# The vector, scalar and GpSimd queues of an MoE and MLP kernel written out by hand, and the gate's short products moved between tiles

## The chip, the cores and the metric

The kernel runs on one core of a Trainium2 chip. The metric is the device time of one execution in microseconds (us), lower is better. The core has five engines that matter here: TensorE (PE, matrix products), VectorE (DVE), ScalarE (ACT), GpSimd (POOL) and SyncE (SP, which issues the DMA transfers). Each engine takes its instructions in a fixed order, and an instruction at the head of a queue that waits for another engine holds back all that stands behind it.

## The reference, cut to what matters

```python
def attention(q, k, v):            # 2 x 8 heads, 576 positions, 64 wide
    out_d = sm_attn(q_d, k_d, v_d) # on means of 4 positions
    out_local = softmax(where(|i - j| < 4, q k^T / 8, -1e9)) @ v
    return repeat(out_d, 4) + out_local

def moe(x, w_gate, w1, w2):        # x: 1152 x 512, 8 experts, hidden 1024, float32
    P = exp(x @ w_gate - max)
    for _ in range(8):
        P /= P.sum(1, keepdims=True) + 1e-09
        P /= P.sum(0, keepdims=True) + 1e-09
        P *= N / E
    return sum(P[:, e:e+1] * (maximum(x @ w1[e], 0) @ w2[e]) for e in range(E))

def mlp(x, w_in, w_out):           # hidden 2048; w_in and w_out are float64
    return log(1 + exp(x @ w_in)) @ w_out
```

The three follow each other: attention gives the MoE's x, the MoE gives the MLP's.

## The kernel before

**Precision.** Each float32 operand is split into a high part (`h`, cut by a cast) and the rest (`l`), and each product is made as three: high by high, high by low, low by high. The splits are the work of ACT (casts), DVE and POOL (subtractions).

**Steps.** The MoE and the MLP are one list of 80 steps, a step being one slice of 256 hidden columns of one expert (the MLP counts as experts 8 and 9) for one of the two sets of tokens: s=0 is four tiles of 128 tokens (half: 256 columns), s=1 five tiles (half: 320). Steps 0 to 3 run beside the attention, the main loop from step 4 (the fifth step); steps 64 to 79 are the MLP. A step has **first products** (`first`, line 577): seven products of a Strassen-like scheme on half blocks, of six matmuls (line 601) each, and **second products** (`second`, line 649), one group of six matmuls of 512 columns (line 660) for each tile. The first products of step n+2 are written between the tiles of step n, so between two of a step's products there is as a rule one tile of second products. Only PE's order is written by hand (`manual_schedule` in the main loop); the queues of DVE, ACT, POOL and SP are set by the scheduler of the framework.

**Between the products.** The first products share three banks of PSUM. Three of them are copied out by ACT (`t1`, `t5`, `u2`: line 610, called the t and u copies below), and PE may write the bank again only after the copy. Three combines on DVE (`c11`, `c22`, `c12`: line 615) add the next products to these copies. `hidden` makes the hidden values: in the MoE a Relu on ACT (line 558, `hh`) and the low part on DVE (line 559, `hl`); in the MLP eight instructions for log(1 + exp(x)) on ACT, DVE and POOL (lines 564 to 575). The second products accumulate in PSUM and are added to the rows with the gate's factor on DVE (`weigh`, line 677).

**Weights.** Each slice of an expert's weights is loaded raw (`raw`, a pool of two buffers) and split: `fetch_first` for w1 (loads `raw<-in_moe_w`, casts lines 132 and 138, subtractions lines 133 and 139, four sums of blocks on POOL, line 111), `fetch_second` for w2 (casts line 153, subtractions line 154). They are issued three slices ahead.

**float64 weights.** `convert` (line 162) turns one of 32 pieces of the float64 weights into float32 high and low parts with integer operations (lines 178 to 189, on `cva`), splits it (lines 196 and 197) and stores it to a scratch in DRAM (`s_in`, `s_out`), from where the MLP steps load it ready. It is called from step 12 on, two pieces in three steps.

**Gate.** `gates` (line 464) makes the logits before the main loop, and nine short products (line 482, `lg`, 18 matmul records) turn them by tiles. Then `sinkhorn` runs in pieces, one after each tile of second products from step 4 on: the row part is four small DVE instructions (lines 503 to 506), then a product on PE sums the columns (line 509, `m<-pr,ones`), and four more on DVE (lines 511 to 516).

**Turn to the MLP.** `again` (line 680) transposes the MoE's result on PE, copies it out on ACT (line 693, `xf`) and makes the seven operands of the first products for each of two halves `kk` (`operands`: casts line 241, subtractions line 242).

Of the kernel before, what the change touches and what calls it, by code (L numbers as in the profile page):

```python
# [20 lines left out]
def attention_moe_mlp(ctx: ExitStack, tc: tile.TileContext, q, k, v, w_gate, w1, w2, w_in, w_out, out):  # L21
# [30 lines left out]
    OPS = 7  # L52

# [6 lines left out]
    tmpp = ctx.enter_context(tc.tile_pool(name="tmpp", bufs=11))  # L60
# [11 lines left out]
    def tmp(s, name):  # L72
        return tmpp.tile([P, HALF[1]], F32, tag="t", name=name)[:, : HALF[s]]
# [29 lines left out]
    weights = {}  # L103
# [9 lines left out]
    def fetch_first(f, n):  # L113
        e, p = divmod(n, NP)
# [7 lines left out]
        raw = rawp.tile([P, 2, 2, 2, P], F32, tag="raw", name="raw1")  # L122
# [5 lines left out]
        for part, src in (  # L128
            (slice(SUMS, SUMS + 1), raw[:, 0:1, :, 0, :]),
            (slice(SUMS + 1, OPS), raw[:, 1].rearrange("p k f c -> p f k c")),  # L130
        ):
            nc.scalar.copy(hi[:, part], src)
            nc.vector.tensor_tensor(lo[:, part], src, hi[:, part].bitcast(F32), op=ALU.subtract)
        two = [smp.tile([P, 2, 2, P], F32, tag="sums", name="sums") for _ in range(2)]
        weight_sums([two[i // 2][:, i % 2] for i in range(SUMS)], lambda fh, d: raw[:, d, :, fh, :])
        for i, sums in enumerate(two):
            part = slice(2 * i, 2 * i + 2)
            nc.scalar.copy(hi[:, part], sums)  # L138
            nc.gpsimd.tensor_tensor(lo[:, part], sums, hi[:, part].bitcast(F32), op=ALU.subtract)  # L139

    def fetch_second(f, n):
# [8 lines left out]
        raw = rawp.tile([P, 2, DM], F32, tag="raw", name="raw2")  # L150
        nc.sync.dma_start(raw, w2[e].rearrange("(h a p) d -> p h a d", h=2, p=P)[:, :, p, :])
        for i in range(2):
            nc.scalar.copy(hi[:, i], raw[:, i])  # L153
            nc.gpsimd.tensor_tensor(lo[:, i], raw[:, i], hi[:, i].bitcast(F32), op=ALU.subtract)  # L154


    TINY = 2.0 ** -15 * 1.125

    HALVES = F2 // P

    def convert(i):

        raw = rawp.tile([P, 2, 2, 2 * P], U32, tag="raw", name="raw64")
# [13 lines left out]
        a = smp.tile([P, SUMS * P], U32, tag="sums", name="cva")  # L177
# [399 lines left out]
    def first(n):  # L577
# [16 lines left out]
        def product(i, b=None):  # L594
            more = b is not None
            if not more:
                b = bank(places[i], f"m{i}")
# [261 lines left out]
```

## Time and profile before

| what | us |
|---|---|
| three runs, median (lowest to highest) | 1095.36 (1095.34 to 1096.3) |
| span of the profiled execution | 1094.7 |
| the median less this span | 0.66 |
| PE busy, share of the span | 1060.0, 97% |
| DVE busy | 727.0, 66% |
| ACT busy | 555.2, 51% |
| POOL busy | 537.6, 49% |

The profiled execution's own time is its span; what lies around it is taken as the 0.66 us by which the median of the runs is longer. PE's busy time counts matmuls that overlap, so idle time, and late starts from one matmul to the next, are what tells of lost time. In the trace, a name in front of `<-` is what an instruction writes and the names behind it what it reads; the bracket at the end is the time that its engine sat idle before it and what ended this.

### The profile page before, as it was taken

The numbers are of one execution on the slowest core, as the hardware profiler recorded it, in microseconds if no ns is written. First come the engines' busy times: TensorE is split into PE (matmuls) and PEld (weight loads), VectorE is DVE, ScalarE is ACT, GpSimd is POOL, SyncE is SP. The second block draws the span as 40 slices with busy tenths as digits, with TensorE's granted clock in tenths as the row PEclk, the third lists the DMA queues.
The fourth block names the chain that finished last, engine by engine and source line by source line (L and its number), as shares of the span: only waits on it lengthen the run. The fifth ranks groups of instructions, "written<-read, shape, count | busy, mean of one in ns | idle before, by whom it ended". The sixth has DMA issues, their size and how long they took to land.

```text
span 1094.7 us, 17873 instructions
## 1 busy us (share of the span) xinstructions
PE 1060.0 (97%) x6385; PEld 938.0 (86%) x6385; DVE 727.0 (66%) x1532; ACT 555.2 (51%) x1443; POOL 537.6 (49%) x569
## 2 busy tenths in 40 slices
PE   6899999999999999999999999999999998999998
PEld 5678888998987889888888988898898897889987
DVE  6889665565666676667657665766663578766765
ACT  4667645343444444434444443444443567676763
POOL 6735235464467676756766455354664212222321
PEclk9579999999999999999999999999999999999999
DMA  8454101111235334434443332223333273244112
GB/s 175 118 115 109 49 27 55 62 58 40 84 100 145 115 110 143 132 105 127 122 134 102 117 112 93 100 93 110 102 116 116 106 278 139 113 175 182 68 39 87
DMA packets 133497, 119.70 MB, mean 109 GB/s; under 512 B 35744, under 2 KB 111776, under 8 KB 133408
## 3 DMA queue, kind: packets, MB, share of 16 engines
q1 hardware_dynamic: 133408, 118.56, 35.0%
q8 instruction: 50, 0.82, 0.3%
q14 instruction: 39, 0.32, 0.1%
HBM read 93.11 MB, written 25.43 MB: 108 GB/s over the span
## 4 chain that ended last, share of the span: by engine, by line
PE 40%; POOL 5%; DMA 5%; DVE 3%; issue 2%; ACT 2%; SPq 0%; POOLq 0%; ACTq 0%; DVEq 0%
PE yps L660 21%; PE m L601 19%; DMA raw<-in_moe_w_out 2%; POOL sums L111 2%; POOL w2l L154 1%; POOL cva L188 1%; POOL cva L197 1%; DMA raw<-in_moe_w 1%; DMA raw<-in_moe_w_in 1%; DVE cva L178 1%; POOL w1l L139 1%; DVE cva L189 0%; DVE cva L179 0%; DVE cva L182 0%; DMA s_out<-cva 0%
## 5 line engine op out<-in xcount | busy, mean ns | idle before, releaser
L601 PE MATMUL m<-xh,w1h 128*128 128x320 f32 (+1 forms) x1120 | 336.6, 301 | 13.1 <-ACT t L610 6.3
L601 PE MATMUL m<-xh,w1l 128*128 128x320 f32 (+1 forms) x1120 | 332.5, 297 | 0.0
L601 PE MATMUL m<-xl,w1h 128*128 128x320 f32 (+1 forms) x1120 | 332.4, 297 | 0.0
L601 PEld LDWEIGHTS m<-xh,w1h 128*128 128x128 f32 x1120 | 212.2, 189 | 38.7 <-ACT t L610 10.8
L601 PEld LDWEIGHTS m<-xl,w1h 128*128 128x128 f32 x1120 | 212.4, 190 | 11.8
L601 PEld LDWEIGHTS m<-xh,w1l 128*128 128x128 f32 x1120 | 212.2, 190 | 0.2 <-issue 0.2
L660 PE MATMUL yps<-w2h,hh 128*128 128x512 f32 x502 | 198.5, 395 | 0.0
L660 PE MATMUL yps<-w2l,hh 128*128 128x512 f32 x502 | 198.4, 395 | 0.0
L660 PE MATMUL yps<-w2h,hl 128*128 128x512 f32 x502 | 195.5, 389 | 0.0
L660 PE MATMUL yps<-w2h,h 128*128 128x512 f32 x436 | 153.3, 393 | 0.0
L615 DVE TENSOR_TENSOR c<-m,t 128x256 f32<-128x256 f32 (+1 forms) x160 | 72.3, 452 | 100.9 <-PE m L601 99.5
L139 POOL TENSOR_TENSOR w1l<-sums,w1h 128x512 fp32r<-128x512 f32 x72 | 95.8, 1345 | 78.2 <-ACT w1h L138 54.4
L571 POOL TENSOR_TENSOR ab<-ab,up 128x320 f32<-128x320 f32 (+1 forms) x64 | 53.9, 843 | 157.2 <-ACT ln L567 109.8
L154 POOL TENSOR_TENSOR w2l<-raw,w2h 128x512 fp32r<-128x512 f32 x72 | 94.9, 1339 | 71.4 <-ACT w2h L153 71.3
L558 ACT ACTIVATE hh<-c 128x256 fp32r<-128x256 f32 (+1 forms) x138 | 60.0, 443 | 125.0 <-DVE c L615 123.3
L559 DVE SCALAR_TENSOR_TENSOR hl<-c,hh 128x256 fp32r<-128x256 f32 (+1 forms) x138 | 91.4, 668 | 35.0 <-ACT hh L558 33.2
L660 PEld LDWEIGHTS yps<-w2h,hl 128*128 128x128 f32 x502 | 94.4, 188 | 21.3
L677 DVE SCALAR_TENSOR_TENSOR acc<-yps,pr,acc 128x512 f32<-128x512 f32 x117 | 86.9, 743 | 29.5 <-PE yps L660 29.4
L660 PEld LDWEIGHTS yps<-w2h,hh 128*128 128x128 f32 x502 | 94.7, 189 | 12.6 <-DVE acc L673 0.2
L660 PEld LDWEIGHTS yps<-w2l,hh 128*128 128x128 f32 x502 | 94.7, 189 | 11.1 <-issue 0.4
L660 PEld LDWEIGHTS yps<-w2h,h 128*128 128x128 f32 x436 | 82.6, 189 | 14.8
L188 POOL TENSOR_TENSOR cva<-cva,raw 128x512 uint32<-128x512 uint32 x32 | 42.7, 1336 | 95.2 <-DVE raw L185 76.6
(134 smaller groups left out, 1700.7 us busy)
## 6 DMA issues: line engine op xcount, KB each, us to landing
raw<-in_moe_w SPq DMA_DIRECT2D x72, 256.0 KB
raw<-in_moe_w SPq DMA_DIRECT2D x36, 512.0 KB
w1h<-s_in SPq DMA_DIRECT2D x10, 896.0 KB
w1l<-s_in SPq DMA_DIRECT2D x10, 896.0 KB
raw<-in_moe_w_in SPq DMA_DIRECT2D x32, 256.0 KB
raw<-in_moe_w_out SPq DMA_DIRECT2D x16, 512.0 KB
w2l<-s_out SPq DMA_DIRECT2D x10, 512.0 KB
w2h<-s_out SPq DMA_DIRECT2D x10, 512.0 KB
```

Source lines behind the costliest of these rows:

```text
L111: nc.gpsimd.tensor_tensor(sums[i], a, b, op=op)
L139: nc.gpsimd.tensor_tensor(lo[:, part], sums, hi[:, part].bitcast(F32), op=ALU.subtract)
L154: nc.gpsimd.tensor_tensor(lo[:, i], raw[:, i], hi[:, i].bitcast(F32), op=ALU.subtract)
L178: nc.vector.tensor_scalar(a, high, 0x07FFFFFF, 3, op0=ALU.bitwise_and, op1=ALU.logical_shift_left)
L188: nc.gpsimd.tensor_tensor(a, a, low, op=ALU.add)
L558: nc.scalar.activation(hh, c, AF.Relu)
L559: nc.vector.scalar_tensor_tensor(out=hl, in0=c, scalar=0.0, in1=hh.bitcast(F32), op0=ALU.max, op1=ALU.subtract)
L571: nc.gpsimd.tensor_tensor(ab, ab, up, op=ALU.subtract)
L601: nc.tensor.matmul(b[:, :h], x[:, i, kk, :], y[s][:, i, kk, :], start=(not more and n == 0), stop=(n == 5), skip_group_check=more,)
L615: nc.vector.tensor_tensor(c, b[:, :h], t, op=ALU.add)
L660: nc.tensor.matmul(y, a[:, f, tok], b[:, f, :], start=(start and m == 0), stop=(stop and m == 5))
L677: nc.vector.scalar_tensor_tensor(out=acc[t], in0=y, scalar=pr[:, t, e : e + 1], in1=acc[t], op0=ALU.mult, op1=ALU.add,)
```

## The change

1. **Queues by hand.** A planner (`Order`, with a `Job` for each chain of instructions) keeps a clock for each engine, in which each instruction has a duration written in the code (0.35 to 1.35 us). After each product and each tile it issues the instructions that, by its clock, can start before PE's next piece is done; on ACT and DVE only those that end within 0.6 us (`SLACK`) after it. The copies and combines that PE's products need are put at their places directly. ACT's, DVE's and POOL's order is fixed in this way from step 4 to step 61 (`turned[1] - 2` is 62); from there the scheduler sets it again. SP stays with the scheduler in the whole kernel.
2. **Conversions.** They begin at step 4 instead of 12, one at a time, as the planner finds room. Two of a conversion's DVE instructions are gone (lines 179 and 185 of before), and one ACT instruction is added (a Copy of the low words with scale 2^-29; its value is added by POOL's addition as before). Per kernel: 64 DVE instructions fewer, 32 on ACT more; POOL, PE and SP as many as before.
3. **Buffers.** The raw pool of two buffers becomes two pools of one: in the main loop the weights use one, the conversions the other (in the attention w1 the one, w2 the other). The conversions' `cva` get a pool of their own (`lowp`), which the MLP's `up` shares; `ln` moves to the pool of the sums.
4. **Gate.** The nine short products go from in front of the main loop to step 4, three after each of three tiles, with a copy after each three; the Sinkhorn pieces begin three tiles later, and in the ninth step (n = 8) two pieces follow each tile.
5. **`again`.** The operands are made for all of the first half `kk`, then all of the second, with every subtraction on DVE.

From the main loop on, PE's order is the same but for the gate's products. In the attention stage the scheduler still sets all queues; with the other pools it comes to another order there (PE's first differs at its 180th row; on SP the loads of w2 stand earlier, those of w1 later), with the same work.

```diff
-    rawp = ctx.enter_context(tc.tile_pool(name="rawp", bufs=2))
+    rawp = [ctx.enter_context(tc.tile_pool(name=f"raw{i}", bufs=1)) for i in range(2)]
...
+    class Order:
+
+        SLACK = 0.6
...
+        def one(self, end):
+            best = None
+            for job in self.jobs:
+                at_ = None if job.active else self.begin(job)
+                if at_ is None:
+                    continue
+                last = end if job.want[0] in ("POOL", "DMA") else end + self.SLACK - job.want[1]
+                key = at_ + 0.25 * job.rank
+                if at_ <= last and (best is None or key < best[0]):
+                    best = key, job
...
+    LOAD, LANDS = 2.0, 2.2
...
+        bits = yield "ACT", 0.69, t
+        nc.scalar.activation(low, low, AF.Copy, scale=2.0 ** -29)
+        t = yield "DVE", 0.6, t
         nc.vector.tensor_scalar(a, high, 0x07FFFFFF, 3, op0=ALU.bitwise_and, op1=ALU.logical_shift_left)
-        nc.vector.scalar_tensor_tensor(
-            out=a, in0=low, scalar=29, in1=a, op0=ALU.logical_shift_right, op1=ALU.bitwise_or
-        )
+        t = yield "DVE", 0.8, t
         nc.vector.scalar_tensor_tensor(
             out=a, in0=high, scalar=0xC0000000, in1=a, op0=ALU.bitwise_and, op1=ALU.bitwise_or
         )
-        nc.vector.tensor_scalar(low, low, 28, 1, op0=ALU.logical_shift_right, op1=ALU.bitwise_and)
...
+    def logits(shares):
+        for t0 in range(0, NTT, LOGITS):
+            lg = spare[0][:, HALF[1] : HALF[1] + LOGITS * E]
+            for t in range(t0, t0 + LOGITS):
+                nc.tensor.matmul(
+                    lg[:, (t - t0) * E : (t - t0 + 1) * E], shares[:, t * P : (t + 1) * P], fold, start=True, stop=True
+                )
+            nc.vector.tensor_copy(prf[:, t0 * E : (t0 + LOGITS) * E], lg)
+            yield
+        nc.vector.tensor_reduce(m1, prf, axis=AX.X, op=ALU.max)
+        yield from sinkhorn()
...
-        for i in ORDER:
-            for kk in range(2):
-                yield from operands(s, kk, xf[kk], (i,), [nc.vector if i in FASTI else nc.gpsimd])
+        for kk in range(2):
+            split[s].append(order_.add(operands(s, kk, xf[kk], ORDER, [nc.vector], order_.free["ACT"]), 1))
...
-    CV = 12
+    CV = 4
...
+                for _ in range(0 if not m else 2 if n == ends[0, 1] + 1 else 1):
```

Three places show what moves (line numbers are each kernel's own: 610 of before is 821 of the change, 615 is 828, 153 is 292, 196 is 346). The first is ACT in front of the first products of step 46, whose t and u copies are the `COPY` rows with 128x320; rows with `raw_` and `cva` are a conversion's, `w2h` are casts of w2. Before:

```order
L558 ACTIVATE h_7313<-c_7355 128x256
L558 ACTIVATE h_7313<-c_7372 128x256
L186 ACTIVATE raw_7423<-raw_7423 128x512
L558 ACTIVATE h_7313<-c_7389 128x256
L558 ACTIVATE h_7313<-m_7315 128x256
L153 CAST w2h<-raw_7417 128x512 x2
L196 CAST raw_7423<-cva 128x512
L610 COPY t_7450<-m_7443 128x320
L610 COPY t_7459<-m_7452 128x320
```

With the change:

```order
L737 ACTIVATE h_7235<-c_7285 128x256
L292 CAST w2h<-raw_7255 128x512 x2
L737 ACTIVATE h_7235<-c_7304 128x256
L737 ACTIVATE h_7235<-c_7326 128x256
L737 ACTIVATE h_7235<-m_7237 128x256
L346 CAST raw_7073<-sums 128x512
L346 CAST raw_7073<-cva 128x512
L821 COPY t_7376<-m_7367 128x320
L821 COPY t_7393<-m_7378 128x320
```

The casts of w2 stand three Relus earlier, and the conversion next to the copies is an older one, at its last two casts, while before it was one whose casts followed on its first instructions in the same step.

The second is DVE at the Sinkhorn pieces beside step 8 (`c_` and `hl` or `h_` rows are the combines and the low parts, `grs` and `pr` the row part, `gcs` and `pr` the column part). Before:

```order
L615 TENSOR_TENSOR c_2796<-m_2789,t_2762 128x256
L559 SCALAR_TENSOR_TENSOR h_2754<-c_2796,h_2753 128x256
L511 TENSOR_REDUCE gcs<-m_2789 128x8
L514 TENSOR_SCALAR gcs<-gcs 128x8
L515 RECIPROCAL gcs<-gcs 128x8
L615 TENSOR_TENSOR c_2820<-m_2755,t_2771 128x256
L516 SCALAR_TENSOR_TENSOR pr<-pr,gcs 128x72
L503 TENSOR_REDUCE grs<-pr 128x9
L504 TENSOR_SCALAR grs<-grs 128x9
L559 SCALAR_TENSOR_TENSOR h_2754<-c_2820,h_2753 128x256
L505 RECIPROCAL grs<-grs 128x9
L506 TENSOR_TENSOR pr<-pr,grs 128x72
```

With the change:

```order
L828 TENSOR_TENSOR c_2955<-m_2946,t_2915 128x320
L739 SCALAR_TENSOR_TENSOR hl<-c_2955,hh 128x320
L680 TENSOR_REDUCE grs<-pr 128x9
L681 TENSOR_SCALAR grs<-grs 128x9
L682 RECIPROCAL grs<-grs 128x9
L683 TENSOR_TENSOR pr<-pr,grs 128x72
L688 TENSOR_REDUCE gcs<-m_2946 128x8
L691 TENSOR_SCALAR gcs<-gcs 128x8
L692 RECIPROCAL gcs<-gcs 128x8
L693 SCALAR_TENSOR_TENSOR pr<-pr,gcs 128x72
L828 TENSOR_TENSOR c_2987<-m_2907,t_2926 128x320
L828 TENSOR_TENSOR c_2996<-m_2917,u_2944 128x320
```

The row part and the column part, which had a combine and a low part between them, now follow each other directly, and PE's product `m<-pr,ones` between them comes right after the tile.

The third is ACT at the turn to the MLP, in front of the first products of step 66 (`xf` are copies of the transposed rows, `xh_` casts of operands, `ab`, `ln` and `hh` hidden values; the copies `t_` are again what PE waits for). Before:

```order
L610 COPY c_9964<-m_9820 128x320
L564 ACTIVATE ab<-c_9964 128x320
L574 CAST hh<-ab 128x320
L565 ACTIVATE ab<-ab 128x320
L567 ACTIVATE ln<-ab 128x320
L610 COPY t_10007<-m_10000 128x320
L610 COPY t_10016<-m_10009 128x320
```

With the change:

```order
L821 COPY c_9941<-m_9797 128x320
L767 CAST hh<-ab 128x320
L932 COPY xf_9872<-tp 128x2x128
L932 COPY xf_9873<-tp 128x2x128
L752 ACTIVATE ln<-ab 128x320
L748 ACTIVATE ab<-ab 128x320
L746 ACTIVATE ab<-c_9941 128x320
L821 COPY t_9984<-m_9977 128x320
L821 COPY t_9993<-m_9986 128x320
L406 CAST xh_103<-xf_9872 128x256
```

The last two copies `xf` now stand behind `c_9941`, and the casts `xh_`, six of which stood among the rows ahead of the t copies, stand behind them: from the first `xf` copy to `t_` there are 21 rows where there were 27.

## Rows read from the trace of the kernel before

**Rows 1.** Windows: stretch, length, busy time of PE, PEld, DVE, ACT, POOL, granted clock.
```profile
0.00:165.00 165.00, 146.70 (x1101) 123.50 (x1101) 126.51 (x345) 102.10 (x388) 79.91 (x108) 0.88 0.44 99
205.00:853.00 648.00, 639.02 (x3680) 568.70 (x3680) 414.09 (x729) 275.75 (x610) 375.03 (x370) 1.00 0.34 107
530.00:660.00 130.00, 129.91 (x759) 116.71 (x760) 86.26 (x150) 57.69 (x128) 75.36 (x72) 1.00 0.38 118
```
**Rows 2.** Windows of line 188 alone (POOL, one instruction in each conversion): length, busy (count).
```profile
530.00:660.00 130.00, 9.28 (x7) 1.00 0.38 118
```
**Rows 3.** Waits of PE, 165 to 853 us: for what, us in total, times, longest.
```profile
PE m L601 <- ACT t L610: 3.9, 6, 1.2
```
**Rows 4.** Timeline of PE at step 46: start, us, instruction, idle before it.
```profile
665.52 0.39 PE L660 MATMUL yps<-w2l,hh 128*128 128x512 f32 x1
665.75 0.39 PE L660 MATMUL yps<-w2h,hl 128*128 128x512 f32 x1
667.35 0.42 PE L601 MATMUL m<-xh,w1h 128*128 128x320 f32 x1 [1.20 <-ACT t L610]
667.60 0.31 PE L601 MATMUL m<-xl,w1h 128*128 128x320 f32 x1
667.75 0.31 PE L601 MATMUL m<-xh,w1l 128*128 128x320 f32 x1
```
**Rows 5.** Timeline of ACT at the same place.
```profile
666.35 0.62 ACT L196 CAST raw<-cva 128x512 fp32r<-128x512 f32 x1 [1.50 <-DVE cva L189]
666.88 0.75 ACT L610 COPY t<-m 128x320 f32<-128x320 f32 x2
```
**Rows 6.** Groups of DVE and ACT by line, 205 to 853 us: busy, mean ns | idle before.
```profile
L178 DVE TENSOR_SCALAR cva<-raw 128x512 uint32<-128x512 uint32 x32 | 28.6, 892 | 49.8 <-DMA raw<-in_moe_w_out 18.3 <-POOL w1l L139 17.4 <-DMA raw<-in_moe_w_in 14.0
L179 DVE SCALAR_TENSOR_TENSOR cva<-raw,cva 128x512 uint32<-128x512 uint32 x32 | 22.5, 702 | 0.7
L186 ACT ACTIVATE raw<-raw 128x512 f32<-128x512 f32 x32 | 21.9, 684 | 53.2 <-DVE cva L182 49.2 <-DMA raw<-in_moe_w 4.0
L558 ACT ACTIVATE hh<-c 128x320 fp32r<-128x320 f32 x57 | 26.1, 470 | 48.9 <-DVE c L615 48.9
L559 DVE SCALAR_TENSOR_TENSOR hl<-c,hh 128x320 fp32r<-128x320 f32 x57 | 42.4, 757 | 13.6 <-ACT hh L558 12.3
L615 DVE TENSOR_TENSOR c<-m,t 128x320 f32<-128x320 f32 x56 | 27.1, 484 | 49.7 <-PE m L601 48.6 <-ACT u L610 1.0
```
**Rows 7.** Line 178 at 339 and 523 us, duration in ns; POOL's timeline there.
```profile
L178 DVE TENSOR_SCALAR cva<-raw x1: 1503/1503/1503, 339.1 to 339.1; 128x512 uint32<-128x512 uint32 x1
...
L178 DVE TENSOR_SCALAR cva<-raw x1: 427/427/427, 523.6 to 523.6; 128x512 uint32<-128x512 uint32 x1
...
337.76 2.52 POOL L139 TENSOR_TENSOR w1l<-sums,w1h 128x512 fp32r<-128x512 f32 x2
...
525.88 1.29 POOL L188 TENSOR_TENSOR cva<-cva,raw 128x512 uint32<-128x512 uint32 x1 [2.80 <-DVE raw L185]
```
**Rows 8.** Chain that ended last, 300 to 700 us: longest landing of a load.
```profile
654.78 4.67 DMA raw<-in_moe_w_out
```
**Rows 9.** Timeline of PE: the nine short products in front of the main loop.
```profile
164.75 2.17 PE L482 MATMUL lg<-fold,lts 16*128 16x8 f32 x18
```
**Rows 10.** Timelines of DVE and PE at a Sinkhorn row part.
```profile
184.52 0.22 DVE L503 TENSOR_REDUCE grs<-pr 128x9 f32<-128x72 f32 x1
...
185.55 0.23 DVE L506 TENSOR_TENSOR pr<-pr,grs 128x72 f32<-128x72 f32 x1
...
185.93 0.30 PE L509 MATMUL m<-pr,ones 128*128 128x72 f32 x1 [0.46 <-DVE pr L506]
```
**Rows 11.** The turn to the MLP: timelines of ACT and PE, then the clock.
```profile
915.08 0.73 ACT L610 COPY t<-m 128x320 f32<-128x320 f32 x2
...
915.54 0.41 PE L601 MATMUL m<-xh,w1h 128*128 128x320 f32 x1 [2.42 <-ACT t L610]
...
916.00:920.00 4.00, 4.00 (x16) 3.68 (x15) 2.42 (x6) 2.28 (x5) 0.82 (x1) 0.57 0.00 0
```

More of the change, by code (lines that the diff above doesn't have):

```diff
@@ L70, in attention_moe_mlp, with tmp @@
     turns = count()
-    def tmp(s, name):
+    held = []
+    class Mark:
+        want = True
+    def tmp(s, name, owner=None):
+        if order_.on:
+            if len(held) >= TEMPS and held[-TEMPS]:
+                old = held[-TEMPS]
+                assert isinstance(old, Job) or not old.want, name
+                order_.force(old)
+            held.append(owner or order_.running)
         return tmpp.tile([P, HALF[1]], F32, tag="t", name=name)[:, : HALF[s]]
@@ L101, in attention_moe_mlp, with __init__, go @@
     s_out = scratch("s_out", [F2 // (2 * P), 2, P, 2, DM])
-    weights = {}
+    weights, fetching = {}, {}
+    class Job:
+        def __init__(self, steps, rank):
+            self.steps, self.rank, self.want, self.active, self.taken, self.done = steps, rank, None, False, {}, set()
+            self.last = 0.0
+            self.go(None)
+        def go(self, value):
+            before, order_.running = order_.running, self
+            self.active = True
+            try:
+                self.want = self.steps.send(value)
+            except StopIteration:
+                self.want = None
+            self.active, order_.running = False, before
@@ L596, in product @@
             if not more:
+                if i == 5 and step - 1 in making:
+                    order_.force(making[step - 1][-1][1])
                 b = bank(places[i], f"m{i}")
+            for job in split[s] if e >= E else ():
+                while job.want and i not in job.done:
+                    order_.step(job)
+                    order_.now = max(order_.now, job.last)
             n = 0
@@ L681, in again @@
     def again(s, banks):
+        assert s or not any(job.taken.get("raw") or job.rank == 2 for job in order_.jobs)
         if s:
@@ L685, in again @@
         else:
-            xf = [rawp.tile([P, 2, 2 * HALF[s]], F32, tag="raw", name="xf2") for _ in range(2)]
+            xf = [x.tile([P, 2, 2 * HALF[s]], F32, tag="raw", name="xf2") for x in rawp]
         for i, t in enumerate(TILES[s]):
@@ L781, in attention_moe_mlp, with conversions @@
     ahead[turned[1] - 2] = [turned[1] - 1, turned[1]]
-    balance, pending, pieces = sinkhorn(), None, 0
+    balance, pending = logits(shares), None
+    def conversions():
+        t = 0.0
+        for e in range(2):
+            for kind in range(2):
+                for i in range(HALVES // 2):
+                    t = yield from convert(kind * HALVES + e * HALVES // 2 + i, t)
     def leading(ns):
@@ L789, in leading @@
             yield from lead(n)
+    others = ExitStack()
     with tc.manual_schedule(engines={mybir.EngineType.PE}):
+        order_.on = True
+        others.enter_context(
+            tc.manual_schedule(engines={mybir.EngineType.Activation, mybir.EngineType.DVE, mybir.EngineType.Pool})
+        )
         for n in range(BESIDE, len(steps)):
+            if n == turned[1] - 2:
+                order_.on = False
+                others.close()
+                for job in order_.jobs:
+                    while job.want:
+                        job.go(0.0)
+                order_.jobs.clear()
+            if n == CV:
+                order_.add(conversions(), 2)
             e, g, s, p = steps[n]
@@ L812, in attention_moe_mlp @@
                     weigh(e, s, i, ys[i])
[L813 to L814 removed]
+                for _ in range(0 if not m else 2 if n == ends[0, 1] + 1 else 1):
+                    if not balance:
+                        break
+                    order_.did("DVE", 0.6)
+                    if next(balance, True):
+                        balance = None
+                        for t in range(NTT):
+                            scaled[t] = order_.add(scale_rows(t))
                 for _ in range(PIECES):
```

244 lines of the change are left out of this document (200 added, 44 removed).

## The prediction

> **What bounds the kernel now.** I read the windows by stage first, then PE's waits, then one wait closely on each engine. In the main stretch, 205 to 853 us, PE is busy 639.02 of 648 us at a granted clock of 1.00 [rows 1]: TensorE is the bound, and what this change could at most give back there is the time in which PE stands. Its printed idle time is 648 - 639.02 = 9.0 us. It isn't spread evenly: from 530 to 660 us PE stood 0.09 of 130 us, and the 130 us from 710 to 840 read the same (130.00 busy). The waits behind the idle time are mostly those for ACT's t and u copies, 3.9 us in six waits for the t copies alone, and then for DVE's combines [rows 3]. So PE does not lack work of its own; a copy comes late now and then.
>
> Why it comes late is to be seen at step 46. PE waits 1.20 us for the t copy [rows 4]. ACT had been idle for 1.50 us before the cast of line 196, which waited for a conversion's instruction on DVE, and the t copies stand right behind this cast [rows 5]. The copy was ready to run; its queue was blocked by work that nobody needs for hundreds of us. In PE's timeline I count 17 late starts of this kind from 205 to 853 us; behind nearly all stands a conversion, or a split of weights, in the queue of ACT or DVE.
>
> A late start costs more than its printed idle time. At step 46 the last second product begins at 665.75 and the next matmul at 667.35, 1.60 later where the pace is 0.23 (665.52 to 665.75): 1.37 lost against 1.20 printed. And the first matmul after the wait takes 0.25 to the next (667.35 to 667.60) where the pace is 0.15 [rows 4]: 0.10 more. So each costs 0.27 over what is printed, and the 17 together 9.0 + 17 x 0.27 = 13.6 us.
>
> **The change part by part.** The sum is made against the span of the profiled execution, 1094.7; the median of the runs is 0.66 above it.
>
> Queues by hand: the mechanism acts at the right place. The planner lets ACT and DVE begin a conversion's instruction only if, by its clock, it ends within 0.6 us after PE's piece, so it should not stand waiting ahead of a t copy. A t copy has a tile and a product's time until PE needs its bank, which is what the order before also gave where nothing stood in front. If all 17 go: -13.6. What remains of them, or comes new, is not in the trace. The bounds: below by 0, since PE's busy time can't shrink; above by 13.6, the same rate as now. The nearest row is the stretch from 530 to 660 us, which had seven conversions in it [rows 2], as has the one from 710 to 840, one in 18.6 us; the changed kernel spreads 32 over some 640 us, one in 20. Those stretches lost 0.1 us, so conversions at this pace fit beside the products if they fall right. But the planner's durations are fixed numbers: it gives line 178 0.6 us, where the trace has a mean of 0.89 [rows 6], and a load 4.2 us to land, where the longest in the chain takes 4.67 [rows 8]. I take 3 us, nearer to the clean stretches than to the rate of now.
>
> Conversions: the removed instruction of line 179 took 0.70 us, 22.5 us in all, and the other removed one comes on top; the added one on ACT is of the size of line 186, 0.68 us, so 32 x 0.68 = 22 us [rows 6]. DVE is busy 414.09 and ACT 275.75 of 648 us [rows 1], so both have room, and neither sum lies on the path: 0. What hides the added ACT work is the idle time of ACT behind PE; where that cover is gone, it is a late t copy of 0.68 us plus 0.27, which is inside the 3 us.
>
> The Trainium skill, "ScalarE: Activation LUTs", "Rules for kernel authors", would have plain arithmetic on DVE rather than ACT; by that rule this edit goes the wrong way. The row of the form on ACT (0.68) is shorter than that of the DVE instruction it replaces (0.70), so the trace doesn't bear the rule out here.
>
> Gate: the nine short products took 2.17 us in front of the loop [rows 9] and take the same between tiles, where PE is the bound too: 0, within the 0.1 of a restart for each of three groups. The Sinkhorn pieces begin three tiles later and are made up in step 8 by two pieces per tile, and there a wait is added: PE's column product comes right after the tile, and needs the row part. Before the row part DVE's queue holds the combine and the low part, which waits for ACT's Relu: 0.48 + 0.47 + 0.76 us [rows 6]. The row part itself ran from 184.52 to 185.78 with a low part of about 0.4 inside [rows 10], so 0.85 to 1.0 alone. From the end of the product this is 2.7 us, and one tile, six times 0.23 = 1.38, runs beside it: PE waits 1.3, and twice so, each with the 0.27: +3.2. Bounds: 0 if the Relu and the low part were passed earlier than the rows say, 5 if the column part also holds back the combines behind it in DVE's queue (c and t banks that PE needs next). The wait at 185.93 (0.46, with its 0.27) goes, as the pieces are elsewhere: -0.7. Together +2.5.
>
> Raw buffers: weights now have one buffer, so a load can't start before the last subtraction of the load before. The price is a rival's, below; the forecast has 0, since one load of weights comes per step (some 53 steps lie in the 648 us, so 12 us each) and holds the buffer for a landing and some 3 us of casts and subtractions.
>
> Turn to the MLP: before, PE waited 2.42 us for the t copies of step 66, which ACT reached only at 915.08, and the clock of 916 to 920 us was 0.57 [rows 11]; so 4 x 0.43 = 1.7 us are lost by the clock behind the wait. In the new order six rows fewer stand ahead of this t copy, at some 0.4 us each, about 2.4 us: the wait goes, and the drop of the clock behind it with it: -(2.42 + 0.27 + 1.7) = -4.4. But the six casts now stand in front of the u copy of the same step, and there I expect a wait of 1.4 and 0.27: +1.7. Net -2.7. Bounds: -4.4 and +2, the second if the u copy's wait is as long as the old one and brings the clock down too.
>
> Attention: PE stands 165 - 146.70 = 18.3 us there, and the clock is 0.88 [rows 1]. The same work comes in another order of loads; nothing in the trace shows it. I take 0 with a bound of 4 us to both sides, somewhat under one landing [rows 8].
>
> Sum: 1094.7 - 13.6 + 3 + 2.5 - 2.7 = 1083.9; with 0.66 it is 1084.6, **1085**.
>
> **The rivals.** A, the forecast: 1085, chance 0.58, own range 1080 to 1090.
>
> B, about a third of the gain goes back because DVE and POOL disturb each other and a fixed order hands each delay on. Line 178 took 1.50 us at 339.05, while POOL's subtractions ran until 337.76 + 2.52 = 340.28, and 0.43 at 523.6, while POOL stood [rows 7]. The 0.6 of the plan is then short by up to 0.9. Price: the mean excess over the undisturbed one is 0.89 - 0.43 = 0.46, with the restart 0.73; if it reaches a combine in 8 of 32 conversions, 5.8 us: 1091. For it speaks that the order can't give way any more; against it that line 178 took 0.89 on average before as well, in the stretches without a loss too. Chance 0.16. The Trainium skill ("SBUF — State Buffer", "Who interferes with whom") says that DVE in a two-port mode, or with two inputs from SBUF, and GpSimd take a shared pair of ports as an exclusive lock, and that the other one blocks fully. The row agrees: line 178 ended 0.27 after POOL's subtractions.
>
> C, no change, 1095: the 17 late starts move rather than go (3 becomes about 13), or the attention stage takes 4 us and the turn to the MLP gives nothing. This includes that the planner's clock is off by more than a piece, so that its places are no better than the scheduler's. Chance 0.11.
>
> D, slower: the single raw buffer. Some 56 loads of weights come from step 4 on, each held until POOL's last subtraction. Where POOL is late by a conversion's chain (one instruction of POOL is 1.3 us [rows 7]), the load starts late, lands up to 4.67 us later, and the cast that waits for it stands in ACT's fixed queue ahead of a t copy. It decides from the point where landing and wait exceed the plan's 4.2 us by the slack of a t copy, about 1.5 us. If 30 of 56 loads then cost 0.8 each, it is +24, so 1085 + 24 = 1109; at half of that, 1097. In between, 1103. Against it: the buffer is taken for 7 to 8 of 12 us. Chance 0.15.
>
> **How the numbers follow.** A measurement of this kernel tells about 0.2%, 2.2 us, from no change, so faster is below 1093.2 and slower above 1097.6. A and B are faster, with a little of both beyond the bound (0.02), which part of C makes good: faster 0.74. C gives most of same: 0.11. D is slower: 0.15. The range leaves out a tenth below and D above: from 1085 - 6 = 1079, with the residual at 0 and the attention stage or the turn better by 3, up to 1096, which holds B and C.
>
> **What would show it right or wrong.** PE's waits for t and u copies and combines from 205 to 853 us should fall from some 9 us to 2 or 3, and PE's idle time in this stretch with them. The column product in step 8 should show two waits of 1.3 us for DVE. At the turn to the MLP the wait for the t copies should be gone, and a shorter one for a u copy there. ACT's casts behind loads of weights should wait little: if they wait over 1.5 us and t copies stand behind them, it is D. If DVE's line of 178 (now followed by one instruction fewer) is longer than 0.9 and combines are late after it, it is B. The forecast is wrong at its root if the idle time stays although no conversion stands ahead of a t copy, or if PE's busy time or its clock in this stretch changes.

## The result, and the profile of the changed kernel

The changed kernel takes 1108.79 us (median of 4 runs, 1103.73 to 1111.51) against 1095.45 for the kernel before: a ratio of 1.012, interval 1.0098 to 1.0142. It is slower by 13 us, where 1085 was forecast. A second set of 6 runs, on the chip of some experiments below, measured 1108.80 (1.0106, 1.0082 to 1.0130).

The profiled execution has a span of 1101.9 us; it is the fastest of the four (1103.73), so its trace holds some 5 us less of the loss than their median. Its windows (stretch, length, busy time of PE, PEld, DVE, ACT, POOL, granted clock, DMA share, GB/s), cut by what happens in them:

```profile
0.00:165.00 165.00, 144.63 (x1091) 120.91 (x1092) 127.03 (x343) 101.72 (x386) 77.47 (x108) 1.00 0.44 99
...
200.00:258.00 58.00, 46.01 (x246) 39.42 (x246) 40.98 (x97) 19.73 (x43) 26.58 (x28) 0.94 0.26 77
258.00:882.00 624.00, 624.00 (x3636) 561.93 (x3635) 375.86 (x620) 291.57 (x644) 370.97 (x355) 1.00 0.35 108
882.00:900.00 18.00, 14.65 (x93) 12.97 (x92) 14.92 (x33) 8.75 (x24) 3.19 (x3) 1.00 0.72 234
```

From 258 to 882 us PE is busy all 624.00 of 624 us. [rows 1] had 9 us of idle time in nearly the same stretch. So what the change is about worked: no idle time of PE is left there. But from 200 to 258 us, where the kernel before had PE busy 58.00 of 58 us, PE now stands 12 us, and the granted clock falls to 0.94.

Where the time goes between the two kernels is read from one fixed point of each step, the start of its last combine on DVE. Here it is for steps 4, 13, 58 and 79, in the kernel before (timeline: start, us, instruction):

```profile
164.38 0.48 DVE L615 TENSOR_TENSOR c<-m,u 128x320 f32<-128x320 f32 x1
...
271.11 0.41 DVE L615 TENSOR_TENSOR c<-m,u 128x256 f32<-128x256 f32 x1
...
820.57 0.47 DVE L615 TENSOR_TENSOR c<-m,u 128x320 f32<-128x320 f32 x1
...
1077.18 0.42 DVE L615 TENSOR_TENSOR c<-m,u 128x256 f32<-128x256 f32 x1
```

and in the changed kernel:

```profile
165.90 0.48 DVE L828 TENSOR_TENSOR c<-m,u 128x320 f32<-128x320 f32 x1
...
291.87 0.42 DVE L828 TENSOR_TENSOR c<-m,u 128x256 f32<-128x256 f32 x1
...
827.28 0.48 DVE L828 TENSOR_TENSOR c<-m,u 128x320 f32<-128x320 f32 x1
...
1084.35 0.42 DVE L828 TENSOR_TENSOR c<-m,u 128x256 f32<-128x256 f32 x1
```

The lag is 1.5 us at step 4, 20.8 at step 13, 6.7 at step 58 and 7.2 at the end. So 19.3 us are lost between steps 4 and 13, 14.1 are won back up to step 58, and the turn to the MLP changes it by 0.5. A second profile of the changed kernel gives 21.5 between steps 4 and 13:

```profile
168.03 0.48 DVE L828 TENSOR_TENSOR c<-m,u 128x320 f32<-128x320 f32 x1
...
296.22 0.42 DVE L828 TENSOR_TENSOR c<-m,u 128x256 f32<-128x256 f32 x1
```

The place of the loss is the gate. PE's waits from 165 to 260 us (what for, us in total, times, longest), where the kernel before had one wait for `pr`, of 0.46 [rows 10], and one of 0.49 for a low part:

```profile
PE m L686 <- DVE pr L683: 9.1, 6, 2.9
PE m L809 <- DVE gcs L688: 2.9, 3, 1.4
PE m L809 <- DVE hl L739: 1.7, 2, 1.2
PE m L809 <- DVE m L670: 0.4, 1, 0.4
```

These twelve waits, 14.1 us, with 0.27 for each restart (3.2, the figure of the sum) and 3.5 for the clock (58 x 0.06), make 20.8; less the 1.5 of the two waits before, that is the 19.3, by this estimate.

The worst of them, in step 8. DVE, then POOL, then PE (timelines):

```profile
245.64 0.49 DVE L739 SCALAR_TENSOR_TENSOR hl<-c,hh 128x320 fp32r<-128x320 f32 x1 [0.54 <-ACT hh L737]
246.05 0.22 DVE L680 TENSOR_REDUCE grs<-pr 128x9 f32<-128x72 f32 x1
246.31 1.18 DVE L681 TENSOR_SCALAR grs<-grs 128x9 f32<-128x9 f32 x1
247.52 0.21 DVE L682 RECIPROCAL grs<-grs 128x9 f32<-128x9 f32 x1
247.77 1.00 DVE L683 TENSOR_TENSOR pr<-pr,grs 128x72 f32<-128x72 f32 x1
...
246.19 2.49 POOL L294 TENSOR_TENSOR w2l<-raw,w2h 128x512 fp32r<-128x512 f32 x2 [2.95 <-ACT w2h L292]
...
248.82 0.70 PE L686 MATMUL m<-pr,ones 128*128 128x72 f32 x2 [2.93 <-DVE pr L683]
```

Two things are to be seen. The row part is the four rows from 246.05, and it starts only after the combine and the low part `hl`, as the prediction had it. But line 681, which works on nine numbers per partition, takes 1.18 us, and line 683 takes 1.00, while GpSimd runs two subtractions of 1.25 us: 681 ends with the first (246.19 + 1.25 = 247.44), 683 with the second (248.68). PE waits 2.93 instead of the 1.3 of the sum. Durations of the gate's DVE instructions over the whole gate (views by line: minimum/median/maximum in ns of eight each):

```profile
L680 DVE TENSOR_REDUCE grs<-pr x8: 218/224/229, 198.8 to 254.0; 128x9 f32<-128x72 f32 x8
...
L681 DVE TENSOR_SCALAR grs<-grs x8: 173/175/1251, 199.1 to 254.3; 128x9 f32<-128x9 f32 x8
...
L682 DVE RECIPROCAL grs<-grs x8: 215/216/217, 199.3 to 255.5; 128x9 f32<-128x9 f32 x8
...
L683 DVE TENSOR_TENSOR pr<-pr,grs x8: 232/728/1210, 199.5 to 255.8; 128x72 f32<-128x72 f32 x8
```

Two of the four never change, two reach five to seven times their shortest. The difference is by kind of instruction, not by size: 681 and 682 work on the same nine numbers. GpSimd was not always at work beside them. Of the 32 instructions of the two kinds that change (16 of them in the column parts), 15 began while a GpSimd instruction ran, and all 15 were held (they had begun, and stood) until 0.03 us (tensor_scalar) or 0.09 us (two inputs) after its end; the 17 others kept their shortest time within 0.01 us. Of the sixteen reciprocals four began in the same way, and took 0.20 to 0.22 us like the rest.

### The profile page after: what moved, and what is told of

It reads as the page before. It is cut to its first block, busy times and chain, and to the rows that moved or that the text cites. A ratio compares the mean times of both kernels' runs of the same rounds, so it can differ in the third digit from the quotient of the medians.

```text
span 1101.9 us, 17721 instructions
## 1 busy us (share of the span) xinstructions
PE 1059.6 (96%) x6385; PEld 939.4 (85%) x6385; DVE 719.1 (65%) x1470; ACT 570.5 (52%) x1475; POOL 545.7 (50%) x569
## 4 chain that ended last, share of the span: by engine, by line
PE 82%; DVE 12%; ACT 2%; issue 1%; POOL 1%; DMA 1%; SPq 0%; DVEq 0%; POOLq 0%; ACTq 0%
PE yps L886 41%; PE m L809 36%; DVE xl L408 2%; PE sc L535 1%; DVE w1l L260 1%; DVE hl L739 1%; DVE ex L549 1%; DVE small L547 1%; DVE c L828 1%; PE pv L591 1%; DVE xf L404 1%; PE tp L569 1%; PE sc L522 1%; PE tb L489 1%; DVE qkd L494 0%
## 5 line engine op out<-in xcount | busy, mean ns | idle before, releaser
L809 PEld LDWEIGHTS m<-xl,w1h 128*128 128x128 f32 x1120 | 212.6, 190 | 13.3 <-DVE xl L408 0.4
L294 POOL TENSOR_TENSOR w2l<-raw,w2h 128x512 fp32r<-128x512 f32 x72 | 99.3, 1398 | 91.8 <-ACT w2h L292 83.8
L739 DVE SCALAR_TENSOR_TENSOR hl<-c,hh 128x256 fp32r<-128x256 f32 (+1 forms) x138 | 95.1, 694 | 33.7 <-ACT hh L737 32.2
L821 ACT COPY t<-m 128x256 f32<-128x256 f32 (+1 forms) x160 | 63.5, 400 | 95.4 <-PE m L809 94.9
```

Source lines behind the costliest of these rows:

```text
L739: nc.vector.scalar_tensor_tensor(out=hl, in0=c, scalar=0.0, in1=hh.bitcast(F32), op0=ALU.max, op1=ALU.subtract)
L809: nc.tensor.matmul(b[:, :h], x[:, i, kk, :], y[s][:, i, kk, :], start=(not more and n == 0), stop=(n == 5), skip_group_check=more,)
L821: nc.scalar.copy(t, b[:, :h])
```

## The experiments

Five theories were at stake. **G**: the moved and doubled gate pieces cost the time as such. **P**: some DVE instructions stand while GpSimd works. **O**: in a queue written out by hand the row part stands behind a combine and low parts, where a scheduler may lift it. **A**: the attention stage pays for the split raw buffers. And, for the turn to the MLP, that the end of the planner crowds DVE. Medians are of 5 to 12 runs, the kernel before on the same chip beside them (1095.6 to 1096.9).

**The gate back in its old place**, everything else as changed:

```diff
-    balance, pending = logits(shares), None
+    balance, pending = sinkhorn(), None
...
-                for _ in range(0 if not m else 2 if n == ends[0, 1] + 1 else 1):
+                for _ in range(1 if m else 0):
```

> The changed kernel with the gate as before: the nine short products in front of the main loop, Sinkhorn pieces one per tile from step 4 on, no doubled pieces in step 8; all else as changed. Theory G (the moved and doubled gate pieces cost the time): the loss of about 20 us between steps 5 and 12 goes, the stall-free stretch stays, so 1085 to 1089. Theory P (the conversions, which begin at step 4 now, put GpSimd's long instructions beside Sinkhorn's small DVE instructions, which wait for them): half of the loss stays, 1093 to 1099.

Measured: 1095.26 (0.9996, 0.9981 to 1.0011), as fast as before and 13.5 below the changed kernel. In its trace the lag between steps 4 and 13 grows by 3.3 us instead of 19.3. PE's waits there, 165 to 260 us:

```profile
PE m L799 <- DVE gcs L678: 0.7, 1, 0.7
PE yps L876 <- POOL w2l L294: 0.3, 1, 0.3
PE m L676 <- DVE pr L673: 0.2, 1, 0.2
```

So without the gate part of the change most of the loss is gone. The small instructions are held here too (12 of the 32, up to 1.13 us, against 15 and 1.26), but PE waits about 1 us for the two parts instead of 12.0: here being held cost time only where PE's product stands right behind. The time came out above what theory G gave for it (1085 to 1089). One reason is in the same trace: between steps 58 and 79 this kernel loses 6.0 us, where the changed one loses 0.5. PE's waits from 850 to 1000 us:

```profile
PE m L799 <- DVE c L818: 4.2, 3, 2.3
PE m L799 <- ACT u L811: 1.6, 1, 1.6
```

The other is the attention stage, below.

**The gate part alone**, put into the kernel before (same edit the other way round):

> The kernel before with the gate part of the change alone: short products in threes in step 4, pieces three tiles later, two per tile in step 8; queues by the scheduler, conversions from step 12. Theory G: 10 to 20 us slower, 1105 to 1115. Theory P: only the two waits of step 8, 1096 to 1099.

Measured: 1099.10 (1.0032, 1.0014 to 1.0050), 3.5 us slower. Between steps 4 and 13 it loses 3.9 us. Theory G falls: alone, the moved gate costs 3.5 us, not 19. With the 3.3 of the run before, which had all but the gate part, some 12 of the 19.3 are left that come only when the two meet.

**Conversions from step 12**:

```diff
-    CV = 4
+    CV = 12
```

> The changed kernel with the conversions beginning at step 12, as before, all else as changed. Theory P: Sinkhorn's chain is free of the conversions' GpSimd instructions, two thirds of the loss between steps 5 and 12 go, so 1090 to 1096, if the conversions still fit. Theory G: the waits for the row part in steps 6 to 8 stay, 1102 to 1109.

Measured: 1130.01, far slower, and useless as a total: the conversions don't finish, and what is left stands in front of the first MLP products, where one wait for a combine takes 27.4 us. Read by stages it tells something: between steps 4 and 13 it loses 14.2 us, against 19.3 and 21.5. So the conversions carry some 5 to 7 us there; their work on DVE and ACT is gone as well as that on GpSimd, so this run doesn't tell which. The wait of 2.9 in step 8 is still there, since what runs beside it on GpSimd is a split of w2 and no conversion. Both theories had their numbers wrong.

**Row parts early.** Each row part is written one piece earlier, behind the column part whose result it needs, so that a whole tile lies between it and PE's product; PE's order is the same:

```diff
+        by_rows()
         for it in range(8):
-            rs = const.tile([P, NTT, 1], F32, tag="grs", name="grs")
...
             yield
             cp = spare[0][:, HALF[1] : HALF[1] + NTT * E]
...
+            if it < 7:
+                by_rows()
             yield
```

> The changed kernel with each Sinkhorn row part written one piece earlier, right behind the column part it depends on; PE's order is the same. Theory O (the fixed DVE queue puts the row part behind a combine and low parts that wait for later products, where the scheduler had put it ahead): the waits of PE for the row part go, the loss of 19 us between steps 4 and 13 shrinks to 7 or less, 1094 to 1099. Theory P (the small DVE instructions wait for GpSimd's long ones wherever they stand): 10 to 14 us of the loss stay, 1100 to 1105.

Measured: 1097.53 (1.0007, 0.9991 to 1.0022), 11.3 us better than the changed kernel on the same chip. Between steps 4 and 13 it loses 12.6 us in the profile, 7 to 9 less than the changed kernel. So theory O's total was met, but the loss that stays is the one that theory P gave (10 to 14), and the rest of the 11.3 is not located. PE's waits for the row part fall from 9.1 to 1.1 us:

```profile
PE m L815 <- DVE gcs L691: 4.8, 3, 2.7
...
PE m L689 <- DVE pr L683: 1.1, 2, 0.6
```

but now PE waits for the column part, which reads the bank that PE must write next. The chain is still on PE's path, at its other end.

**GpSimd kept short during the gate.** Its subtractions and additions of weights and conversions work on 8 columns instead of 512 while the gate is balanced, so the kernel leaves out most of these low parts; DVE's and ACT's order is the changed kernel's:

```diff
-            nc.gpsimd.tensor_tensor(lo[:, i], raw[:, i], hi[:, i].bitcast(F32), op=ALU.subtract)
+            nc.gpsimd.tensor_tensor(lo[:, i, k], raw[:, i, k], hi[:, i, k].bitcast(F32), op=ALU.subtract)
```

> The changed kernel with GpSimd's subtractions and additions of weights and conversions cut to 8 columns while the gate is being balanced (the low parts of these weights and pieces are left out, the high parts stand in their place in the products); the four sums of blocks stay. Order on DVE, ACT and PE as changed. Theory P: the small DVE instructions fall to about 0.2 us each, the two waits in step 8 to 1.3 us, the loss between steps 4 and 13 to 8 or less, 1094 to 1100. Theory O: 14 or more of the 19 us stay, 1103 to 1108.

Measured: 1093.10 (0.9960, 0.9941 to 0.9978), 15.7 us better than the changed kernel on the same chip, with the gate's pieces where they were. Between steps 4 and 13 it loses 5.6 us. The same place in step 8:

```profile
240.68 0.22 DVE L689 TENSOR_REDUCE grs<-pr 128x9 f32<-128x72 f32 x1
240.94 0.17 DVE L690 TENSOR_SCALAR grs<-grs 128x9 f32<-128x9 f32 x1
241.14 0.22 DVE L691 RECIPROCAL grs<-grs 128x9 f32<-128x9 f32 x1
241.39 0.24 DVE L692 TENSOR_TENSOR pr<-pr,grs 128x72 f32<-128x72 f32 x1
...
241.69 0.44 PE L695 MATMUL m<-pr,ones 128*128 128x72 f32 x2 [1.17 <-DVE pr L692]
```

The 1.18 and 1.00 us have become 0.17 and 0.24, with nothing changed on DVE, and PE waits 1.17. That is the wait the prediction had worked out (1.3). Theory P holds: 14 of the 19 us (16 of the 21.5) hang on GpSimd. O has a part in it, since a wait needs both a held chain and a PE that stands right behind it. With the row parts early the small instructions are held as often as in the changed kernel (17 of the 32), but PE's waits for the two parts are 5.9 us instead of 12.0; with the gate back about 1; with GpSimd short 3.7. No run has both ways out in the changed gate, so how far their gains add up is not shown.

**The raw buffers in turn in the attention stage**, as before the change, on three kernels: the changed one, the one with row parts early, the one with the gate back:

```diff
-        raw = rawp[0].tile([P, 2, 2, 2, P], F32, tag="raw", name="raw1")
+        raw = rawp[0 if order_.on else next(rawturn) % 2].tile([P, 2, 2, 2, P], F32, tag="raw", name="raw1")
```

> The changed kernel with the raw buffers taken in turn in the attention stage, as before (w1 and w2 alternate), all else as changed. Theory A (the attention stage lost by the split of the raw pool, some 1.5 us at equal or better clock, up to 8 at the clock of before): 1098 to 1105. Theories G and P: no change, 1103 to 1110.

> The row parts early, and the raw buffers taken in turn in the attention stage, as before the change. If the split of the raw pool costs the attention stage time (theory A), 3 to 6 us less than with the row parts early alone; if not, the same within 1.5 us.

> The gate as before the change and the raw buffers in turn in the attention stage, all else as changed. If both costs are independent (theories P and A): 1095.3 less some 5.6, so 1088 to 1091.5, faster than the kernel before. If the buffers only helped together with the row parts: 1094 to 1096.

> The changed kernel once more, on the same chip as these others: 1104 to 1111, as in the first runs. With the buffers in turn (the run before this set) at 1102.7 on another chip, theory A expects this to stay at 1106 or more; if it comes at 1102 to 1104, the buffers made no difference.

Measured: 1102.67 (1.0048, 1.0030 to 1.0066); 1091.95 (0.9965, 0.9948 to 0.9982); 1088.82 (0.9919, 0.9897 to 0.9940); the changed kernel again 1108.80. Against their partners that is 6.1, 5.6 (same chip) and 6.4 us less, three times outside the intervals. So the split of the raw pool cost 5.6 to 6.4 us; the edit acts in a stage that the forecast had put at 0.

Single profiles don't show it in the time at which the stage ends, which differs by some us from execution to execution of one kernel, with clocks from 0.5 to 1.00 in it. But PE's busy time shows it: up to the last combine of step 4, PE stands 19.6 to 23.4 us in the six profiles with the split and 14.0 to 18.5 in the six with the buffers in turn. For the row parts early without and with the edit, 0 to 165 us (columns as in the windows above):

```profile
0.00:165.00 165.00, 143.33 (x1098) 120.48 (x1098) 127.58 (x345) 101.31 (x387) 78.91 (x108) 0.96 0.45 99
...
0.00:165.00 165.00, 149.17 (x1084) 125.26 (x1085) 119.21 (x342) 101.72 (x386) 79.87 (x108) 0.83 0.45 99
```

These are 5.8 us more of busy time, at a lower clock. One instruction stands behind most of it. At 49 us of the changed kernel, DVE and POOL:

```profile
49.21 4.71 DVE L547 TENSOR_SCALAR small<-small 96x3 f32<-96x3 f32 x1
...
48.68 1.41 POOL L226 TENSOR_TENSOR sums<-raw 128x256 f32<-128x256 f32 x2
50.05 0.72 POOL L226 TENSOR_TENSOR sums<-raw,sums 128x256 f32<-128x256 f32 x1
50.73 2.48 POOL L294 TENSOR_TENSOR w2l<-raw,w2h 128x512 fp32r<-128x512 f32 x2
53.17 0.72 POOL L226 TENSOR_TENSOR sums<-raw,sums 128x256 f32<-128x256 f32 x1
...
55.29 0.91 PE L591 MATMUL pv<-et,vw 72*64 72x64 f32 x12 [3.60 <-DVE small L547]
```

and the same line in the pair from above, without the edit (PE waits for the product `ex` that is made from it) and with it:

```profile
48.88 4.45 DVE L547 TENSOR_SCALAR small<-small 128x3 f32<-128x3 f32 x1
...
54.74 1.18 PE L560 MATMUL tp<-ident,ex 96*72 96x96 f32 x6 [4.87 <-DVE ex L549]
...
49.05 0.19 DVE L548 TENSOR_SCALAR small<-small 128x3 f32<-128x3 f32 x1
```

It looks like P once more: an instruction on three numbers per partition, 0.13 to 0.17 us where GpSimd is idle, stands for 4.71 us while six instructions of GpSimd follow each other without a pause, sums of w1 and splits of w2, and ends 0.03 us after the last. In all six profiles with the split (this one, the run again, the gate back, conversions from 12, rows early, GpSimd short) the longest instruction of this line takes 4.45 to 4.86 us, in the six with buffers in turn 1.23 to 2.63, and in the kernel before 1.22. The wait of PE behind it is 3.6 to 5.3 us in all six with the split. With the buffers in turn the longest wait there is 1.8 or less in five profiles, and 2.85 in the sixth, which the trace puts down to ACT. So it carries most of the 6 us; that GpSimd is what holds it is read from the trace alone, as GpSimd was not cut short in this stage, and the other places of the stage were not tested one by one.

**GpSimd kept short at the turn to the MLP** (steps 59 to 63), on the kernel with row parts early and buffers in turn:

> Row parts early and buffers in turn, with GpSimd's subtractions and additions of weights and conversions cut to 8 columns in steps 59 to 63 (what they would have made is left out, high parts in their place). Theory P for the two waits of 1.8 and 1.7 us for DVE's combines at the turn to the MLP: both go, 3 to 4 us less than the 1092.0 without the cut, so 1087.5 to 1089.5. Rival (the planner's end at step 62 empties its jobs into DVE's queue, whatever GpSimd does): the waits stay, 1091 to 1093.

Measured: 1087.19 (0.9927, 0.9901 to 0.9954), 4.8 us less than without (on another chip; the two intervals just touch). Between steps 58 and 79 its trace wins 3.2 us where that without the cut loses 0.5. PE's waits from 850 to 1000 us, without the cut:

```profile
PE m L816 <- DVE c L835: 3.9, 3, 1.7
PE m L816 <- ACT t L828: 0.4, 1, 0.4
```

and with it:

```profile
PE m L825 <- DVE c L844: 0.7, 1, 0.7
PE m L825 <- ACT t L837: 0.4, 1, 0.4
```

The two long waits for combines are gone, so the end of the planner alone does not make them. Up to the first of them DVE's order is the same in both kernels, so that one is GpSimd's. Behind it DVE's order differs in ten places, so for the second GpSimd's part is not isolated. In the changed kernel the combine at 884.57 stood behind two instructions that were held:

```profile
881.22 1.52 DVE L739 SCALAR_TENSOR_TENSOR hl<-c,hh 128x256 fp32r<-128x256 f32 x1
882.66 1.58 DVE L408 TENSOR_TENSOR xl<-xf,xh 128x320 fp32r<-128x320 f32 x1
884.16 0.48 DVE L404 TENSOR_TENSOR x<-xf 128x320 f32<-128x320 f32 x1
884.57 0.41 DVE L828 TENSOR_TENSOR c<-m,t 128x256 f32<-128x256 f32 x1
```

**Towards a better kernel.** The gate back, buffers in turn, and conversions from step 6; then the same with row parts early:

> The gate as before, buffers in turn, conversions from step 6. With fewer of GpSimd's instructions beside the gate, theory P expects 1 to 2 us less than with conversions from step 4: 1087 to 1090; otherwise the same as that run.

> The gate as before the change, row parts early, buffers in turn, conversions from step 6: the parts that helped so far together. In the version without early row parts PE still loses 0.3 to 1.3 us at four places in steps 6 to 12; theory O expects these to go: 1086 to 1088. Theory P expects nothing, since the small instructions then wait for GpSimd at another place: 1088 to 1090.

Measured: 1088.18 (0.9921, 0.9904 to 0.9939) and 1086.59 (0.9917, 0.9888 to 0.9946). Both beat the kernel before and the changed one. Between the two, and against 1088.82 with conversions from step 4, the intervals overlap, so neither of the last two edits is shown to help. The last one stands 0.8% below the kernel before. In its stretch from 258 to 850 us PE is busy all the time as well. What it still loses is the turn to the MLP: 5.4 us between steps 58 and 79, as all kernels with the gate back lose 4.7 to 6.0 there.

## Why the prediction was wrong, point by point

| step of the sum | forecast, us | measured, us |
|---|---|---|
| late starts of the main stretch, net of what remains | -13.6 + 3 | -14.1 (steps 13 to 58) |
| gate and Sinkhorn | +2.5 | +19.3 (steps 4 to 13), 21.5 in the second profile |
| turn to the MLP | -2.7 | +0.5 (steps 58 to 79) |
| attention stage | 0, bound 4 | +5.6 to +6.4 (three pairs of kernels) |
| one raw buffer for weights in the loop | 0 | 0 (no idle time from 258 to 882) |

With 19.3 for the gate this sums to 11.3 to 12.1 us, with 21.5 to 13.5 to 14.3; the medians differ by 13.3.

**The bound was right, and its cause fits.** The 14.1 us won bear out the price of the late starts worked out from [rows 4], printed idle time plus 0.27 (13.6 in all). That the conversions ahead of the copies [rows 5] were the cause fits as well: with them at other places in the queue the stretch has no gap, in every kernel with the queues by hand. No run parts the order from the two DVE instructions fewer and the other buffers. The residual of 3 us was too much; it is 0. The clean stretch in [rows 1] and [rows 2] was the right row to go by, and the planner's short 0.6 us for line 178 did no harm: its successor still reaches 1.52 us at worst, in a stretch where PE never waits. The prediction's comparison of ACT's form with the DVE one that it replaces (0.68 against 0.70) set one input against two: line 178, with one, takes 0.43 on DVE undisturbed [rows 7]. Neither lay on PE's path.

**The step that failed is the Sinkhorn term, by size and not by place.** It stood at +2.5 and measured 19.3 to 21.5. The two waits of step 8 were forecast at their place, with the right queue ahead of them, and with GpSimd kept short they measure 1.17 and 1.15 against the 1.3 of the sum; in the changed kernel they are 2.93 and 2.86. What the step left out is that the four small instructions were priced at their undisturbed durations, [rows 10], with a low part among them but no GpSimd beside them. The wait in [rows 7] had shown what GpSimd does to such an instruction, and rival B was built on it; but B asked where a *conversion's* instruction would reach a combine, 5.8 us, and not which *short* chain lies on PE's path. Up to 1.26 us in place of 0.2, at two of the four instructions of each row and column part, weighs more there than 0.46 on a conversion that nobody waits for. With GpSimd short, 5.6 of the 19.3 us are left, 2.9 of them the two waits of step 8 with their restarts, where the sum had 3.2. The Trainium skill, "SBUF — State Buffer", "Who interferes with whom", tells which instructions are at risk: a tensor_scalar, if its operands allow a mode with two ports, or one with two inputs from SBUF may wait for a whole GpSimd instruction, a tensor_reduce on this chip never. The trace agrees where it can tell: 681 and 683 take up to 1.25 us, and the column part's tensor_reduce (688) 0.22 to 0.23 in all eight, three of which began while GpSimd ran; 680 never began so. Read against the gate's list of instructions, not the conversion's, it would have pointed at the two that are held. The tensor_scalar that was held through six GpSimd instructions, in the attention stage, goes beyond the page's one.

The second omission in the same step: pieces were counted one by one only in step 8. Before the doubled pieces, between 200 and 238 us and with one piece per tile, PE waits for the two parts as well, 6.2 us in seven waits, among them 1.19 and 1.38 up to 207.05 and 208.87. With GpSimd short and the same order 1.4 of this is left, all of it for the column part; so here too most is GpSimd's, and the order alone makes the smaller share. And in this stretch the granted clock was 0.94 over 58 us, about 3.5 us by estimate, which the sum had only at the turn.

**The attention stage** was put at 0 because nothing in the trace showed a cost, with a bound of 4 us from "one landing". The cost is 6, and most of it isn't a landing: PE waits for a chain on DVE that stands while GpSimd's instructions for two loads follow each other without a pause. The rival that shared out one buffer (D) looked at the main loop, where it cost nothing.

**The turn to the MLP.** The wait of 2.42 us in [rows 11] went, with its drop in the clock, as forecast; the forecast new wait for a u copy didn't come (0.4 for a t copy), but two for combines of 1.8 and 1.6, the first by GpSimd. In step terms the changed kernel loses 3.5 us from step 58 to 63, wins 3.9 from there to 70, and loses 0.9 behind it. In the kernels with the gate back PE waits 2.3 us in step 66 again, for a combine, with the drop in the clock in three of four profiles, and 1.6 for a u copy as forecast. So this term depends on how the scheduler's order falls.

**The sign** was wrong, with 0.15 for slower, and that on D, which played no part. The gain was real and 14 us, and was given back nearly twice over, for the most part by DVE's instructions held beside GpSimd: in the gate and, for one wait, at the turn this is shown by cutting GpSimd short; in the attention stage it is read from the trace.

## What to carry to other kernels

When order is taken from a scheduler and fixed by hand, look first for chains of short instructions with PE directly behind them, and put as much of PE's work as there is between chain and product; held instructions that PE does not stand behind cost almost nothing here (with the gate back 12 of 32 were held, for about 1 us of waits). Price each instruction of such a chain by its duration beside GpSimd, not by its median, if it is of a kind that waits for GpSimd. And a gain in one stage says nothing on a change as a whole: compare a fixed point of each step in both traces, and the sum falls into its parts.

## What the runs showed of the hardware that was not expected

- A DVE instruction on 3 numbers per partition stood 4.71 us through six GpSimd instructions in a row: it did not get in between two of them, which followed each other without a pause. That is not the rule of this trace: in the gate eight held instructions got in at the end of the first, though the next followed as closely (681 at 246.31, before the second subtraction). What makes the difference stays open.
- Which instructions wait is a matter of kind: over the eight row parts the reciprocal took 215 to 217 ns and the reduction 218 to 229, while the tensor_scalar went from 173 to 1251 and the two-input product from 232 to 1210. Each of the latter two was held whenever a GpSimd instruction ran as it began, and never otherwise; of the eight reciprocals three began so.
- In the new gate's stretch the granted clock went to 0.94 over 58 us (0.88 in the second profile), where PE stood again and again, up to 2.93 us at a time; it read 0.57 from 238 to 242 us, behind waits of 0.46 and 1.23, and 0.59 from 248 to 252, at the end of the longest. With GpSimd short, where the longest wait is 1.17, it stayed at 1.00.
